# GpSimd takes shifted copies, and both score slots get a third PSUM bank, in a two-layer transformer kernel

## The chip, the cores and the metric

One NeuronCore of a Trainium2 chip runs the whole kernel. The metric is the time of one execution on the device, in microseconds (us). The work is spread over five engines: TensorE (PE in the profile, its weight loads PEld), VectorE (DVE), ScalarE (ACT), GpSimd (POOL) and the DMA queue of SyncE (SP). Each engine runs its own instructions strictly in the order in which they were written, and waits on semaphores for the others.

## The reference

Sequence length 2048, width 512, 32 heads of 16, hidden width 1792; everything bfloat16. The same attention block and the same MLP are applied twice.

```python
def _A_ref(x, wqkv, wo):
    qkv = (x @ wqkv).reshape(B, S, 3, H, Dh) ...
    scores = jnp.einsum("bhqd,bhkd->bhqk", q, k) * (Dh ** -0.5)
    p = _softmax(scores, axis=-1)
    o = jnp.einsum("bhqk,bhkd->bhqd", p, v)
    return o ... @ wo
x = x + _A_ref(_layernorm(x), A_wqkv, A_wo)
x = x + _B_ref(_layernorm(x), B_w1, B_b1, B_w2, B_b2)   # h = gelu(x @ w1 + b1); h @ w2 + b2
x = x + _A_ref(_layernorm(x), A_wqkv, A_wo)
x = x + _B_ref(_layernorm(x), B_w1, B_b1, B_w2, B_b2)
```

## The kernel before, in words

**Cells.** Attention is worked in cells. A cell is one row quarter `a` of the array, one block of 128 keys and 512 query columns: one matmul (`score`, L1137) fills one PSUM bank of 128x512 float32 with transposed scores, an exponential turns the bank into bfloat16 weights in SBUF, and a second matmul (`pvs`, L1527) with 17 columns of V (16 and a column of ones, for the softmax's denominator) adds them to the output bank. There are 4096 cells, grouped in passes of one query segment and one group of heads.

**Two ways to the exponential.** Most cells go to ScalarE (`exps`, L1466), which does two or three banks in one ACTIVATE. Cells of four chosen key blocks per layer (`KD`) can go to VectorE instead. There the exponential is made from integer arithmetic: `dfirst` (L1283) evicts the bank with one multiply and add into uint16, so that the integer is the bit pattern of a bfloat16 near the exponential. `dchain` then makes three shifted copies of it in SBUF, for one cell or a pair of cells: L1344 writes copy 1 (+32) from copy 0, L1346 writes copies 2 and 3 (+64) from copies 0 and 1. The four copies meet V and three scaled versions of V (`vc`) in four second matmuls, and their sum is the better approximation. So a cell on VectorE costs one eviction, its share of two copies, and four second matmuls instead of one.

**Banks.** PSUM has eight banks. Score slot 0 has banks 0, 1 and 2, slot 1 has banks 3 and 4, bank 5 collects the second matmuls of one pass, and banks 6 and 7 are for side work: projections, the MLP's matmuls, the output projection. Bank 7 (and bank 6, when no side work asks for it) may be lent to VectorE's cells. `scores` fills the two slots in turn, and ScalarE works on one while TensorE fills the other. `attach` adds VectorE's cells in lent banks to the group of score matmuls that fills a slot; `swap` gives the third bank of slot 0 to VectorE if VectorE is about to be free. Then ScalarE's ACTIVATE on that slot covers two banks, and the slot becomes free when both ScalarE and VectorE have read it (`slot_done`). Slot 1 is always two banks wide.

**Who writes the order.** A planner in the kernel (`_Sched.run`) holds a thread for each piece of work, a cost for each operation and a clock for each engine, and picks the operation that can start first; ties go by priority. What it picks is appended to that engine's list, with the waits that its reads and writes need (`_Prog.group`). The chip then runs these five lists as they stand: the planner's clocks decide the order and nothing else. Side work is let in when a due share of the cells has been scored (`when`, `HB`, `YB`, `JB`); `fill` puts extra matmuls into gaps on TensorE. `EARLY` is the number of head groups of layer 1's second query segment that are begun before the last key blocks of layer 1 are there. `norm` transposes a finished pass into the tile `XT`, takes reciprocals (L746), multiplies (L754, on GpSimd for most passes, else on VectorE) and transposes back (L759). GpSimd also makes the masked queries (L1085), the normalised rows (L602), the scaled V (L1068) and the layer norm's power (L588).

Of the kernel before, what the change touches and what calls it, by code (L numbers as in the profile page):

```python
# [5 lines left out]
ALU = mybir.AluOpType  # L6
# [14 lines left out]
PVB = 5  # L21
MISC = (6, 7)
# [9 lines left out]
DU = 9  # L32
# [11 lines left out]
EARLY = 4  # L44
# [17 lines left out]
CPRIO = 8  # L62
FPRIO = 1.5
# [11 lines left out]
SHIFT = 32  # L75
# [128 lines left out]

LATENCY = {"pe": 0.20, "act": 0.10, "dve": 0.10, "pool": 0.15, "sp": 0.1}


class _Sched:
# [5 lines left out]
    def __init__(self, P):  # L214
# [10 lines left out]
        self.filler, self.free, self.fills = None, None, set()  # L225

# [70 lines left out]

    def landed(self, keys):
        return max(self.end.get(self.P.lastw[k], 0.0) if k in self.P.lastw else 1e9 for k in keys)
# [34 lines left out]
    def run(self):  # L334
        while True:
# [8 lines left out]
            for th in self.threads:  # L344
# [6 lines left out]
                best.setdefault(e, []).append((th, rdy))  # L351
# [33 lines left out]
            if e == "pe":  # L385
                self.mode = op.mode
                self.note(start + cost - op.cost, start + cost, op)
            self.ops.append((e, start, cost, op.writes[0] if op.writes else ""))
# [113 lines left out]
class _Plan:  # L502
# [215 lines left out]
    def norm(self, l, seg, g, b, part, final):  # L718
# [18 lines left out]
        xt = T["XT"]  # L737
        if part:
# [9 lines left out]
        gb, ts = self.heads(seg, g)  # L748
        o = gb % 2
        pool = g < 6 and seg[2] == 512  # L750
        nb = w // 32
        for i, t in enumerate(ts):
# [4 lines left out]
                reads=["XT", "RC"], writes=["OTT.%d.%d" % (o, t)])  # L757
        if ts[-1] == 1:
            yield _Op("dve", 0.05 + 0.65 * w / 512, lambda e: e.transpose(T["OTN"][:, gb, q0:q0 + w], T["OTT"][:, o, 0:w]),  # L759
                      reads=["OTT.%d.0" % o, "OTT.%d.1" % o],  # L760
                      writes=["OTN.%d.%d" % (gb, t % 4) for t in self.tiles(seg)])
            yield ("give", ("otn", l, seg, gb))
# [262 lines left out]
    def route(self, name, b):  # L1025
# [3 lines left out]
        if self.lend == 2:  # L1029
            return "misc"  # L1030
        return "misc" if q > (0 if b == MISC[0] else QUEUE if self.scored < self.rush else RUSH) or b == MISC[0] else "dbank"

    def setup_attention(self):
# [19 lines left out]
        self.lead = [min(pi for pi, p in enumerate(self.pas) if p[0] == l) for l in range(NL)]  # L1053
        self.held, self.users = [len(x) for x in SLOTS], [0] * len(SLOTS)
# [5 lines left out]
    def vcopies(self):  # L1060
        T = self.T
        for l in range(NL):
# [9 lines left out]
            self.lend = 1  # L1072

# [16 lines left out]
    def free(self, now, ahead):  # L1090
# [3 lines left out]
        for b in (6, 7, 0, 1, 2, 3, 4, 5) if src else ():  # L1094
# [97 lines left out]
    def swap(self, op, start, cells, extra, free):  # L1192
# [11 lines left out]
        f, r = self.score(c, self.s.tokens[("qp", c[0])], SLOTS[0][2])  # L1204
# [8 lines left out]
        self.join(op, d, SLOTS[0][2], extra, free)  # L1213
# [22 lines left out]
    def scores(self):  # L1236
        u = 0
        pools = self.s.pools
        while True:
            sl = yield ("acq", "s")  # L1240
            cells = []
            for _ in SLOTS[sl]:
# [6 lines left out]
            work = list(zip(cells, SLOTS[sl]))  # L1249
# [12 lines left out]
            op.late = lambda op, start: (self.attach(op, start, cells, extra, free), self.swap(op, start, cells, extra, free))  # L1262
# [359 lines left out]
```

The softmax here doesn't subtract the row's maximum and nothing guards it: scores larger than these inputs give would overflow.

## Time and profile before

| what | value |
|---|---|
| median of 3 runs | 1588.41 us (1587.63 to 1589.98) |
| the profiled execution's own time | 1589.16 us |
| its span in the profile | 1587.3 us |
| ScalarE busy | 1547.1 us, 97% of the span |
| TensorE busy | 1424.2 us, 90% |
| VectorE busy | 1352.0 us, 85% |
| GpSimd busy | 200.5 us, 13% |
| granted TensorE clock | 0.995 |
| cells on ScalarE, on VectorE | 3207, 889 |

The cells come from the counts of the groups: 711, 96 and 82 evictions at L1283 make 889, and the rest of 4096 is ScalarE's. Busy times of one engine overlap at their ends: an ACTIVATE's record is longer than the distance to the next one's start, so the distance from start to start tells what one costs.

### The profile page before, as it was taken

The numbers are of one execution on the slowest core, as the hardware profiler recorded it, in microseconds if no ns is written. First come the engines' busy times: TensorE is split into PE (matmuls) and PEld (weight loads), VectorE is DVE, ScalarE is ACT, GpSimd is POOL, SyncE is SP. The second block draws the span as 40 slices with busy tenths as digits, with TensorE's granted clock in tenths as the row PEclk, the third lists the DMA queues.
The fourth block names the chain that finished last, engine by engine and source line by source line (L and its number), as shares of the span: only waits on it lengthen the run. The fifth ranks groups of instructions, "written<-read, shape, count | busy, mean of one in ns | idle before, by whom it ended". The sixth has DMA issues, their size and how long they took to land.

```text
span 1587.3 us, 42896 instructions
## 1 busy us (share of the span) xinstructions
PE 1424.2 (90%) x18701; PEld 444.6 (28%) x18701; DVE 1352.0 (85%) x2564; ACT 1547.1 (97%) x1393; POOL 200.5 (13%) x250
## 2 busy tenths in 40 slices
PE   8998888899999898988989998888998889898988
PEld 3222222222222222222222222222222222333344
DVE  5689999888898889978788789899878988998984
ACT  7999999999999999999999999999999999999996
POOL 5200012001100201002120020122001000010000
PEclk9999999999999999999999999999999999999999
DMA  5100001241114311143111510001251105312520
GB/s 140 22 2 1 2 14 41 77 132 46 27 45 130 85 41 28 42 140 74 36 28 48 172 44 28 1 2 33 67 167 43 28 15 151 103 36 87 155 82 29
DMA packets 141767, 96.88 MB, mean 61 GB/s; under 512 B 36877, under 2 KB 141582, under 8 KB 141582
## 3 DMA queue, kind: packets, MB, share of 16 engines
q1 hardware_dynamic: 141582, 94.14, 21.2%
q8 instruction: 149, 2.44, 0.6%
q14 instruction: 36, 0.29, 0.1%
HBM read 84.41 MB, written 2.10 MB: 55 GB/s over the span
## 4 chain that ended last, share of the span: by engine, by line
ACT 67%; PE 29%; DVE 2%; POOL 1%; issue 1%; DMA 0%; ACTq 0%; POOLq 0%
ACT pt L1466 60%; PE ps L512 11%; PE ps L1137 9%; PE ps L1527 8%; ACT g L893 3%; ACT v L1466 2%; ACT kt L1466 1%; ACT q L1466 1%; DVE du L1283 1%; ACT L893 1%; ACT L1466 0%; DMA xf<-xln 0%; PE ps L1125 0%; POOL xln L602 0%; POOL rstd L588 0%
## 5 line engine op out<-in xcount | busy, mean ns | idle before, releaser
L1466 ACT ACTIVATE pt<-ps 128x1536 bf16<-128x1536 f32 (+2 forms) x1261 | 1384.2, 1246 | 15.2 <-PE ps L1137 10.3
L1137 PE MATMUL ps<-qp,kt 32*128 32x512 bf16 x4096 | 538.0, 385 | 140.8 <-ACT pt L1466 106.7
L1283 DVE TENSOR_SCALAR du<-ps 128x512 uint16<-128x512 f32 x711 | 479.7, 685 | 97.5 <-PE ps L1137 89.6
L1527 PE MATMUL ps<-pt,v 128*17 128x512 bf16 (+1 forms) x3368 | 433.8, 359 | 2.3 <-ACT pt L1466 0.8
L1527 PE MATMUL ps<-du,vc 128*17 128x512 bf16 (+1 forms) x2394 | 333.8, 358 | 2.7 <-DVE du L1346 1.4
L1137 PEld LDWEIGHTS ps<-qp,kt 32*128 32x128 bf16 x4096 | 140.6, 91 | 685.9 <-ACT pt L1466 304.2
L1346 DVE TENSOR_SCALAR du<-du 128x2048 uint16<-128x2048 uint16 x361 | 246.3, 687 | 2.5
L1085 POOL TENSOR_SCALAR qp<-q,mask 128x512 bf16<-128x512 bf16 (+1 forms) x91 | 66.3, 728 | 1013.8 <-PE ps L1137 1005.1
L512 PE MATMUL ps<-xf,wr 128*32 128x512 bf16 (+1 forms) x2400 | 170.8, 368 | 1.7 <-DMA xf<-xln 1.1
L1527 PE MATMUL ps<-du,v 128*17 128x512 bf16 (+1 forms) x798 | 154.7, 360 | 1.7 <-DVE xt L743 0.9
L1344 DVE TENSOR_SCALAR du<-du 128x1024 uint16<-128x1024 uint16 x361 | 150.5, 428 | 2.0
L1527 PEld LDWEIGHTS ps<-pt,v 128*17 128x17 bf16 x3368 | 111.8, 89 | 113.0 <-issue 72.9
L512 PE MATMUL ps<-wr,g 128*32 128x512 bf16 x1600 | 123.8, 384 | 5.5 <-ACT g L893 5.0
L1527 PEld LDWEIGHTS ps<-du,vc 128*17 128x17 bf16 x2394 | 92.5, 89 | 62.7 <-issue 27.5
L872 DVE TENSOR_SCALAR g<-ps,hb1t 128x512 bf16<-128x512 f32 (+1 forms) x112 | 79.8, 713 | 13.8 <-PE ps L512 12.9
L1527 PE MATMUL ps<-dh,vc 128*17 128x512 bf16 (+1 forms) x321 | 90.6, 358 | 0.0
L1283 DVE TENSOR_SCALAR dh<-ps 128x512 uint16<-128x512 f32 x96 | 65.8, 685 | 11.5 <-PE ps L1137 10.8
L1283 DVE TENSOR_SCALAR kt<-ps 128x512 uint16<-128x512 f32 x82 | 56.1, 684 | 20.7 <-PE ps L1137 19.9
L512 PEld LDWEIGHTS ps<-xf,wr 128*32 128x32 bf16 x2400 | 53.6, 95 | 61.5 <-issue 33.5
L602 POOL TENSOR_SCALAR xln<-x,rstd,nmr 128x512 bf16<-128x512 bf16 x58 | 58.2, 1008 | 33.3 <-DMA xf<-xln 23.2
L754 POOL TENSOR_TENSOR ott<-xt,rc 128x256 bf16<-128x256 f32 x42 | 29.5, 703 | 178.5 <-DVE rc L746 178.5
L1125 PE MATMUL ps<-vc 128*32 128x512 bf16 x476 | 50.9, 395 | 0.1
(93 smaller groups left out, 1185.2 us busy)
## 6 DMA issues: line engine op xcount, KB each, us to landing
wr<-in_B_w_dram SPq DMA_DIRECT2D x256, 256.0 KB, 2.9
wr<-in_A_wqkv_dram SPq DMA_DIRECT2D x24, 256.0 KB, 2.9
wr<-in_A_wo_dram SPq DMA_DIRECT2D x18, 256.0 KB, 2.9
out_dram<-x SPq DMA_DIRECT2D x16, 128.0 KB, 2.7
g<-in_A_wqkv_dram SPq DMA_DIRECT2D x3, 512.0 KB, 5.1
x<-in_A_x_dram SPq DMA_DIRECT2D x3, 512.0 KB, 8.0
q<-in_B_w_dram SPq DMA_DIRECT2D x3, 512.0 KB, 3.9
kt<-in_B_w_dram SPq DMA_DIRECT2D x4, 256.0 KB, 3.3
```

Source lines behind the costliest of these rows:

```text
L512: return [lambda e, a=a: e.matmul(out[32 * a:32 * a + 32, :], lhsT=lhsT[:, 32 * a:32 * a + 32], rhs=rhs, start=start, stop=stop, tile_posi ...
L602: yield _Op(eng, cost, lambda e: e.tensor_scalar(T["XLN"][:, x, :], T["X"][:, t, :], T["RSTD"][:, t:t + 1], T["NMR"][:, t:t + 1], op0=ALU. ...
L872: yield _Op("dve", 0.21 + n / 966, lambda e, fc=fc, pb=pb: e.tensor_scalar(T["G"][:, fc, q], pb, T["HB1T"][:, fc:fc + 1], None, op0=ALU.ad ...
L893: lambda e, g=g: e.activation(out=g, in_=g, func=ACT.Gelu_apprx_tanh), reads=gk, writes=gk, prio=2)
L1085: yield _Op("pool", 0.1 + 0.6 * w / 512, lambda e, s=s, q=q, i=i, t=t, w=w: e.tensor_scalar(T["QP"][:, s, w * i:w * i + w], q, T["MASK"][: ...
L1125: fns.append(lambda e, o=o, w=w, a=a, m=m: e.matmul(o, lhsT=w, rhs=rhs, start=start, stop=start, tile_position=(0, m * a)))
L1137: return (lambda e: e.matmul(o, lhsT=lhsT, rhs=rhs, start=True, stop=True, tile_position=(32 * a, 0)), ["K%d.%d.%d" % (l, gb, kt // 4), "Q ...
L1283: yield _Op("dve", 0.68, lambda e: e.tensor_scalar(u, self.bank(b), E_SCALE, E_BIAS, op0=ALU.mult, op1=ALU.add), reads=["B.%d" % b], write ...
L1344: yield _Op("dve", 0.08 + 0.14 * n, lambda e: e.tensor_scalar(U[:, 1, 0:n, :], U[:, 0, 0:n, :], SHIFT, None, op0=ALU.add), reads=key[0], w ...
L1346: yield _Op("dve", 0.08 + 0.28 * n, lambda e: e.tensor_scalar(U[:, 2:4, 0:n, :], U[:, 0:2, 0:n, :], 2 * SHIFT, None, op0=ALU.add), reads=k ...
L1466: yield _Op("act", 0.065 + 0.4267 * n, lambda e, src=src, dst=dst: e.activation(out=dst, in_=src, func=ACT.Exp, scale=0.25), reads=["B.%d" ...
L1527: op.fns.append(lambda e, o=o, lhsT=q[0][0][m], rhs=q[0][1][:, n * m:n * m + n], a=a, st=st, sp=sp: e.matmul(o, lhsT=lhsT, rhs=rhs, start= ...
```

## The change

It has five parts, all in the planner's input; the operations themselves stay, but for the engine of one.

1. **Shifted copies on GpSimd.** Copy 1 (L1344 before, L1381 after) is written for GpSimd when GpSimd's planned clock is more than 0.5 us behind VectorE's (`SPARE`), else for VectorE. Copies 2 and 3 (L1346, then L1384) stay on VectorE (`WHOLE` is False). An eviction is L1318 after, an exponential L1508, a second matmul L1569.
2. **Locks in the plan.** `locking` and `unlocked` keep windows in which GpSimd's operations, and VectorE's SBUF-to-SBUF copies, are taken to exclude each other; such an operation's start is put off to the end of the other's window, so another one may be picked first.
3. **Banks.** Slot 0 keeps 0, 1 and 2. Slot 1 keeps 3 and 4 and gets bank 5 once the first scaled V is made (`widen`). The collecting bank is 6. Bank 7 is left for side work and for VectorE. `swap` may give the third bank of either slot to VectorE.
4. **Norm.** `XT` and the two halves of `OTT` are taken and given back as a whole, so that one pass's norm doesn't begin in them while another's is being planned.
5. **`EARLY`** goes from 4 to 2.

The diff, cut to its core:

```diff
-PVB = 5
-MISC = (6, 7)
+WIDE = 5
+PVB = 6
+MISC = (7, 5)
...
-EARLY = 4
+EARLY = 2
...
+SPARE = -0.5
+WHOLE = False
...
+HOLD = (0.05, 0.13)
...
+    def locking(self, op):
+        w = op.writes[0] if op.writes else ""
+        if op.eng == "pool":
+            return not w.startswith("RSTD")
+        return op.eng == "dve" and (w.startswith("XLN") or w.startswith("DU") and w.split(".")[2] != "0")
+
+    def unlocked(self, op, rdy):
+        if op.eng not in self.locks or not self.locking(op):
+            return rdy
+        now = t = max(rdy, self.clock[op.eng])
+        for a, b in self.locks["pool" if op.eng == "dve" else "dve"]:
+            if a <= t < b and not (op.eng == "dve" and a >= self.fast[0] and t < self.fast[1] + 0.02):
+                t = b
+        return t if t > now else rdy
...
-                best.setdefault(e, []).append((th, rdy))
+                best.setdefault(e, []).append((th, self.unlocked(th.op, rdy)))
...
+            if self.locking(op):
+                self.fast = (start, start + cost) if e == "dve" else self.fast
+                self.locks[e] = self.locks[e][-3:] + [(start + HOLD[0], start + cost - HOLD[1])]
...
+        gb, ts = self.heads(seg, g)
+        yield ("acq", "xt")
...
+        if ts[0] == 0:
+            yield ("take", ("ott", o))
...
+        yield ("rel", "xt", 0)
...
+            yield ("rel", "ott", o)
...
+        if b == WIDE:
+            return "wide"
...
+        self.slots = [list(x) for x in SLOTS]
...
+            if WIDE in self.s.pools["misc"]:
+                self.s.pools["misc"].remove(WIDE)
+                self.s.pools["wide"].append(WIDE)
...
-        f, r = self.score(c, self.s.tokens[("qp", c[0])], SLOTS[0][2])
+        f, r = self.score(c, self.s.tokens[("qp", c[0])], self.slots[sl][2])
...
-        if b in MISC:
+        if b == MISC[0]:
             yield ("rel", "dbank", b)
         else:
-            yield from self.slot_done(0)
+            yield from self.slot_done(0 if b < 3 else 1)
...
-        yield _Op("dve", 0.08 + 0.14 * n, lambda e: e.tensor_scalar(U[:, 1, 0:n, :], U[:, 0, 0:n, :], SHIFT, None, op0=ALU.add),
+        clock = self.s.clock
+        eng, fix, one = ("pool", 0.1, 0.65) if clock["pool"] < clock["dve"] + SPARE else ("dve", 0.08, 0.14)
+        yield _Op(eng, fix + one * n, lambda e: e.tensor_scalar(U[:, 1, 0:n, :], U[:, 0, 0:n, :], SHIFT, None, op0=ALU.add),
                   reads=key[0], writes=key[1])
...
+    def widen(self):
+        yield ("acq", "wide")
+        self.slots[1].append(WIDE)
...
+        s.spawn(self.widen(), 4)
```

## The prediction

> **What bounds the kernel now.** I read the busy times first, then the groups by form, then the order of ScalarE's instructions in time, then the waits, and last the spread of durations of single tiles.
>
> ```profile
> PE 1424.2 (90%) x18701; PEld 444.6 (28%) x18701; DVE 1352.0 (85%) x2564; ACT 1547.1 (97%) x1393; POOL 200.5 (13%) x250
> ACT 67%; PE 29%; DVE 2%; POOL 1%; issue 1%; DMA 0%; ACTq 0%; POOLq 0%
> ```
>
> ScalarE is busy 97% of the span and holds two thirds of the chain that ended last. TensorE's 29% of the chain is mostly stretches in which it runs without a gap beside ScalarE. The exponentials, kept apart by form:
>
> ```profile
> L1466 ACT ACTIVATE pt<-ps 128x1024 bf16<-128x1024 f32 x769 | 798.2, 1080 | 7.4 <-PE ps L1137 6.0
> L1466 ACT ACTIVATE pt<-ps 128x1536 bf16<-128x1536 f32 x491 | 740.2, 1507 | 7.8 <-PE ps L1137 4.2 <-PE ps L1527 1.3
> ```
>
> With those that write into kt, v and q there are 540 three-bank and 793 two-bank ACTIVATEs, and one of one bank. Their records overlap, so the cost is read from start to start, in the timeline of ScalarE:
>
> ```profile
> 346.30 1.48 ACT L1466 ACTIVATE kt<-ps 128x1536 bf16<-128x1536 f32 x1
> 347.63 1.07 ACT L1466 ACTIVATE pt<-ps 128x1024 bf16<-128x1024 f32 x1
> 348.53 1.51 ACT L1466 ACTIVATE kt<-ps 128x1536 bf16<-128x1536 f32 x1
> 349.87 11.48 ACT L1466 ACTIVATE pt<-ps 128x1024 bf16<-128x1024 f32 x10
> ```
>
> 347.63 - 346.30 = 1.33 and 348.53 - 347.63 = 0.90. Over the whole trace the medians are 1.331 and 0.904 us: a bank costs 0.427 us and an instruction 0.05 us. What lies above these medians is a bubble. I summed it: 42.3 us behind two-bank and 4.6 us behind three-bank ACTIVATEs, 47 us in all. A two-bank one covers TensorE's turn (free slot, scores, semaphore) badly, a three-bank one nearly always.
>
> ```profile
> PEld ps L1137 <- ACT pt L1466: 304.2, 598, 2.0
> PEld ps L1137 <- DVE du L1283: 89.6, 152, 1.6
> DVE du L1283 <- PE ps L1137: 89.6, 180, 3.1
> ```
>
> The scores wait mostly for ScalarE (304 us). VectorE has 235 us of idle time, most of it waiting for scores, so it isn't the bound. Outside the exponentials there are 12.3 us before the first one and 26.7 us after the last.
>
> **What the Trainium skill says.** "SBUF — State Buffer", section "Who interferes with whom": VectorE in a two-port mode and GpSimd share a port pair; whoever issues first has it and the other fully blocks. The trace agrees:
>
> ```profile
> L1344 DVE TENSOR_SCALAR du<-du x361: 228/418/1067, 68.7 to 1557.5; 128x1024 uint16<-128x1024 uint16 x175, 128x512 uint16<-128x512 uint16 x6
> L1346 DVE TENSOR_SCALAR du<-du x361: 382/683/1107, 70.2 to 1557.9; 128x2048 uint16<-128x2048 uint16 x175, 128x1024 uint16<-128x1024 uint16 x6
> L1283 DVE TENSOR_SCALAR du<-ps x711: 646/690/694, 65.6 to 1554.5; 128x512 uint16<-128x512 f32 x178
> L1085 POOL TENSOR_SCALAR qp<-q,mask x91: 476/694/1487, 12.7 to 1492.4; 128x512 bf16<-128x512 bf16 x75, 128x256 bf16<-128x256 bf16 x16
> ```
>
> The columns are minimum, median and maximum in ns. Copies go from 418 to 1067 and from 683 to 1107, GpSimd's masked queries from 694 to 1487. "VectorE: DVE Perf Modes", section "Why PSUM operands drop a tier", says that a PSUM operand leaves only one port; so evictions shouldn't block, and they never pass 694. "GPSIMD Engine Reference", section "3.1 Elementwise", gives some 1.8 cycles an element as the best case, 768 ns for 512 elements; the trace has 694 for L1085 there.
>
> **The change part by part.** The counts come from the order of instructions that the changed planner writes.
>
> *ScalarE's work.* VectorE's cells go from 889 to 921, so ScalarE's from 3207 to 3175. There are now 599 three-bank and 689 two-bank ACTIVATEs: 599 x 1.331 + 689 x 0.904 = 1420.2, against 540 x 1.331 + 793 x 0.904 + 0.8 = 1436.4. That is -16.2 us, on the bound. The gelus, table loads and copies are as before.
>
> *VectorE.* Of 512 first copies 357 go to GpSimd (313 of 1024 elements, 44 of 512). VectorE's first copies fall from 194.9 us (150.5 + 27.2 + 17.2 in three groups) to 96 x 0.418 + 59 x 0.284 = 57. The 32 new evictions cost 32 x 0.685 = 22, the extra second copies some 11. Sum -105 us, worth nothing by itself: VectorE is off the path. It is what lets 32 more cells in.
>
> *GpSimd.* No row of before shows this copy. From 256 to 512 elements L1085 goes from 482 to 694 ns undisturbed, so 1024 take 1.12 us by that slope; the page's 1.8 cycles at the 1.2 GHz it states give 1.54 us. I take 1.3 between them: 313 x 1.3 + 44 x 0.7 = 438 us, and GpSimd goes from 200 to some 640 us, 41%. Masked queries and normalised rows now queue behind copies; they are made well ahead (L1085 idled 1005 us for a free buffer), so nothing is late.
>
> *The port.* Before, 123 copies on VectorE met a GpSimd operation begun earlier, and by their means (548, 777 and 305 ns against 417, 682 and 283) lost 13.5 us. GpSimd's busy time grows 3.2 times, its operations (0.8 us on average, the copies 1.3) some 1.5 times in length, VectorE's copies fall from 996 to 667. Unplanned that makes 13.5 x 3.2 x 1.5 x 0.67 = 43 us; if the planned windows hold, nearly nothing. It hits VectorE, not ScalarE.
>
> *The new wait.* L1384 must now wait on VectorE for GpSimd's copy, and the evictions queued behind it wait too; those evictions free score banks. Between the eviction that releases a copy and the wait for it the new order puts a median of 2.9 us of VectorE work. If the copy lands 1.2 us after its release, the places with less cover cost 14 us of VectorE's time; at 1.8 us, 49 us.
>
> *Gated slots, the disputed term.* Before, 124 of 1334 slot turns waited for a VectorE eviction in the slot's own third bank. Behind a two-bank ACTIVATE such turns had a mean bubble of 92 ns (27 of 124 were released late by VectorE), the others 45 ns; behind a three-bank one the mean was 7 ns, none of them gated. Afterwards 671 turns that follow an exponential are gated: 368 behind two banks, 303 behind three; ungated are 321 and 296. The bounds for a gated turn are 45 (the gate is harmless) and 92 behind two banks, 7 and 54 behind three (the same 47 on top, though 0.43 us more cover should take over half of it: 25). I take 70 and 15, since VectorE is less loaded but less punctual: 321 x 0.045 + 368 x 0.070 + 296 x 0.007 + 303 x 0.015 = 46.8 us. Against 46.9 that is nothing. The low bounds give 35 us (-12); 92 and 25 give 58 (+11), 92 and 54 give 67 (+20).
>
> *One bank for side work.* Its 272 evictions and the matmuls before them now take turns in bank 7. In the opening two places in the new order become late: the score group after cell 151 waits for the eviction of the first keys of chunk 3 (two projection groups of eight matmuls, 0.45 us each by the 108 in 6.01 us near the end of the chain, a second copy of 0.68 and the eviction of 0.69 stand in front, and one ACTIVATE of 0.9 covers them), and after cell 199 an exponential waits for second matmuls behind a V eviction. About 2 and 1.5 us, +3.5. At the turn to layer 1 the keys of chunk 3 stand 72 cells ahead of their first use (164 before), which at 0.378 us a cell (1548 us from the first exponential to the last, over 4096) is 27 us, so `EARLY` = 2 costs nothing; without that cover a post-processing chain would stand on the path.
>
> *TensorE.* 102 more second matmuls, four at a time in 0.22 us, are 5.6 us beside 944 fillers of some 95 us: hidden. After the last exponential 12 more stand ahead of the last transpose, +0.6.
>
> *Norm.* Taking `XT` whole delays one pass's transpose at most until the last one's multiply; passes are some 24 us apart. Nothing.
>
> Sum: -16.2 - 0.1 + 3.5 + 0.6 = -12.2 us. The profiled execution took 1589.16 us (its span 1587.3 and 1.9 around it) and lies 0.75 above the median, so: 1589.2 - 12.2 = 1577.0, less 0.75, 1576.
>
> **The rivals.** (1) *The gate is harmless*: VectorE has 105 us more room and hits its marks. Bubbles 35 us, sum -24, 1564. For it: 33 of 60 gated turns that VectorE released last had no bubble. (2) *The gate at its full price*, 92 and 25: bubbles 58 us, sum -1, 1587, the same within measurement (0.2%, 3.2 us, is about what can be told from no change). (3) *Slower: VectorE stands behind GpSimd.* A copy on GpSimd lands late or holds the port, L1384 stands at the head of VectorE's queue, the eviction behind it comes late and with it either slot; both slots are open to it now, one before. VectorE's lateness is up to 49 + 43 = 92 us. My sum stays a gain until 12 us of it reach ScalarE (13%); at a quarter, 23 us, the time is 1599. For it: copies reach 1.1 us where they meet GpSimd. Against: a slot's eviction has most of the other slot's ACTIVATE as slack. That the change doesn't do what it says is excluded by the order: 357 copies stand on GpSimd, banks 2 and 5 have 334 and 341 evictions.
>
> **How the numbers follow.** My forecast, around 1576 (1569 to 1585): 0.45. Rival 1: 0.24. Rival 2: 0.10. Rival 3: 0.21. Faster by over 0.2% is the first two, 0.69; within 0.2% 0.10; slower 0.21. The range goes from 1560, some 4 us under rival 1, to 1595, into rival 3, and leaves out the rest.
>
> **What would show it.** Right: 1288 exponentials at unchanged 1.33 and 0.90 us from start to start, bubbles of 40 to 55 us, GpSimd busy some 640 us, evictions at 690 ns still. Wrong: copies on GpSimd over 1.8 us; VectorE waits for GpSimd of over 50 us; bubbles behind gated turns well above 92 ns; or an idle stretch of ScalarE at the turn to layer 1.

## The result and the profile after

The changed kernel takes 1730.67 us (median of 4 runs, 1727.22 to 1733.69) against 1588.66 us for the kernel before on the same chip: a ratio of 1.0893, 95% interval 1.0868 to 1.0918. It is 9% slower, and far outside the predicted range of 1560 to 1595. The profiled execution took 1733.69 us, its span is 1731.9, the granted clock 0.963.

Busy times and the shares of the chain that ended last, of the kernel after:

```profile
PE 1460.2 (84%) x18803; PEld 439.6 (25%) x18803; DVE 1356.4 (78%) x2263; ACT 1551.6 (90%) x1347; POOL 1175.7 (68%) x605
...
DVE 31%; POOL 28%; PE 24%; ACT 14%; issue 2%; DMA 1%; SPq 0%; POOLq 0%; DVEq 0%; ACTq 0%
```

ScalarE held 67% of the chain before and holds 14% now. GpSimd went from 1% to 28%, VectorE from 2% to 31%. GpSimd is busy 1176 us where some 640 were forecast. The spread of durations (minimum, median, maximum in ns) of the copies and evictions, from the tile `du` after:

```profile
L1318 DVE TENSOR_SCALAR du<-ps x741: 630/682/693, 66.5 to 1696.8; 128x512 uint16<-128x512 f32 x186
L1384 DVE TENSOR_SCALAR du<-du x375: 384/694/2985, 71.4 to 1702.0; 128x2048 uint16<-128x2048 uint16 x183, 128x1024 uint16<-128x1024 uint16 x5
L1381 POOL TENSOR_SCALAR du<-du x291: 1486/2771/3652, 68.4 to 1700.5; 128x1024 uint16<-128x1024 uint16 x142, 128x512 uint16<-128x512 uint16 x4
```

This is the line to read first. A first copy on GpSimd takes 2.77 us in the median, not 1.3. Where nothing of VectorE lay beside them, 1024 elements took 2.77 and 512 took 1.49 us, which is 2.50 ns an element and 0.21 us fixed. VectorE's evictions stay at 0.68 us and never pass 693 ns, but its second copies (L1384) now reach 2985 ns, 1107 before. That longest one is a single case, and no copy of GpSimd's made it: it met the one MEMSET with which GpSimd fills a column of V. From the timelines of the two engines (start, length):

```profile
237.63 2.98 DVE L1384 TENSOR_SCALAR du<-du 128x2048 uint16<-128x2048 uint16 x1
237.78 2.29 POOL L561 MEMSET v<- 128x512 bf16 x1
```

No other copy on VectorE is more than 0.87 us over its undisturbed length. Next the waits of the kernel after (who waits, for whom: us in total, times, longest):

```profile
PEld ps L1172 <- ACT pt L1508: 180.8, 349, 1.9
PEld ps L1172 <- DVE du L1318: 176.2, 266, 2.9
...
DVE du L1384 <- POOL du L1381: 137.5, 112, 2.9
ACT pt L1508 <- PE ps L1172: 128.0, 185, 3.2
...
PEld ps L1569 <- POOL du L1381: 52.9, 60, 2.3
```

The third line didn't exist before: with the same wait on the tiles `kt` and `dh`, VectorE stands 151 us for GpSimd's copies, and 168 us for GpSimd in all. The scores now wait nearly as long for VectorE's evictions (176 us, 90 before) as for ScalarE, and ScalarE waits for scores: 128 us on this row. The last line is a second way for the delay: TensorE's second matmuls stand for GpSimd's copies themselves, and scores are queued behind them. How it goes in one place, from the timeline of VectorE (start, length, in brackets the idle time before and its releaser):

```profile
701.74 0.68 DVE L1318 TENSOR_SCALAR du<-ps 128x512 uint16<-128x512 f32 x1
703.66 0.69 DVE L1384 TENSOR_SCALAR du<-du 128x2048 uint16<-128x2048 uint16 x1 [1.25 <-POOL du L1381]
704.27 0.75 DVE L901 TENSOR_SCALAR g<-ps,hb1t 128x512 bf16<-128x512 f32 x1
704.93 0.68 DVE L1318 TENSOR_SCALAR du<-ps 128x512 uint16<-128x512 f32 x1
```

GpSimd's copy ran from 700.86 for 2.77 us to 703.63. VectorE had 1.35 us of other work in that time (701.07 to 702.42), then stood 1.25 us at L1384; the eviction at 704.93 stood behind it. A stretch of the chain a little later shows this reaching ScalarE (start, length, what):

```profile
712.58 2.92 POOL du L1381
715.50 1.46 POOL dh L1381
716.96 6.37 POOL du L1381 x2
723.35 0.69 DVE du L1384
724.04 0.60 DVE du L1318
724.64 0.67 DVE g L901
725.36 1.05 PE ps L536 x16
726.40 0.35 PE ps L1172 x3
726.77 3.29 ACT pt L1508 x3
```

Four copies back to back on GpSimd (10.75 us), then what stood behind the last of them: the second copy on VectorE, an eviction and an MLP bias (`g`) queued after it, the MLP matmuls that needed that, the scores behind these on TensorE, and the exponential.

ScalarE's time, summed from start to start as in the prediction, tells where the 144.6 us of span (1731.9 - 1587.3) are:

| us | before | after |
|---|---|---|
| exponentials at 1.331 and 0.904 | 1436.4 | 1420.1 |
| bubbles behind two banks | 42.3 | 128.4 |
| bubbles behind three banks | 4.6 | 76.4 |
| after the last exponential | 26.5 | 29.1 |

The 16 us of saved work are there. Bubbles took 158 us. Of those after, 121 are longer than 0.6 us and hold 140 us; before there were 10 with 9 us.

### The profile page after: what moved, and what is told of

It is laid out like the page before. It is cut to its first block, busy times and chain, and to the rows that moved or that the text cites. A ratio compares the mean times of both kernels' runs of the same rounds, so it can differ in the third digit from the quotient of the medians.

```text
span 1731.9 us, 43259 instructions
## 1 busy us (share of the span) xinstructions
PE 1460.2 (84%) x18803; PEld 439.6 (25%) x18803; DVE 1356.4 (78%) x2263; ACT 1551.6 (90%) x1347; POOL 1175.7 (68%) x605
## 4 chain that ended last, share of the span: by engine, by line
DVE 31%; POOL 28%; PE 24%; ACT 14%; issue 2%; DMA 1%; SPq 0%; POOLq 0%; DVEq 0%; ACTq 0%
POOL du L1381 23%; ACT pt L1508 13%; DVE du L1318 10%; DVE du L1384 9%; PE ps L536 9%; PE ps L1569 8%; PE ps L1172 7%; POOL kt L1381 3%; DVE g L901 2%; DVE dh L1384 1%; DVE kt L1384 1%; DVE du L1381 1%; POOL xln L626 1%; DVE kt L1318 1%; DVE dh L1318 1%
## 5 line engine op out<-in xcount | busy, mean ns | idle before, releaser
L1508 ACT ACTIVATE pt<-ps 128x1024 bf16<-128x1024 f32 (+1 forms) x1215 | 1384.2, 1238 | 142.5 <-PE ps L1172 128.0
L1381 POOL TENSOR_SCALAR du<-du 128x1024 uint16<-128x1024 uint16 (+1 forms) x291 | 827.4, 2848 | 371.5 <-DVE du L1318 349.9
L1172 PE MATMUL ps<-qp,kt 32*128 32x512 bf16 x4096 | 524.9, 394 | 146.2 <-ACT pt L1508 69.0
L1318 DVE TENSOR_SCALAR du<-ps 128x512 uint16<-128x512 f32 x741 | 497.2, 682 | 88.0 <-PE ps L1172 84.9
L1569 PE MATMUL ps<-pt,v 128*17 128x512 bf16 (+1 forms) x3330 | 449.9, 369 | 21.4 <-POOL du L1381 10.4
L1384 DVE TENSOR_SCALAR du<-du 128x2048 uint16<-128x2048 uint16 (+1 forms) x375 | 312.9, 840 | 138.2 <-POOL du L1381 137.5
L1569 PE MATMUL ps<-du,vc 128*17 128x512 bf16 (+1 forms) x2487 | 358.0, 371 | 24.0 <-DVE du L1384 14.8
L1569 PE MATMUL ps<-du,v 128*17 128x512 bf16 (+1 forms) x829 | 162.7, 371 | 21.9 <-POOL du L1381 13.2
L1569 PEld LDWEIGHTS ps<-pt,v 128*17 128x17 bf16 x3330 | 112.1, 89 | 145.8 <-issue 76.5
L1569 PEld LDWEIGHTS ps<-du,vc 128*17 128x17 bf16 x2487 | 94.3, 90 | 91.1 <-DVE du L1384 30.8
L1381 POOL TENSOR_SCALAR kt<-kt 128x1024 uint16<-128x1024 uint16 x29 | 84.2, 2904 | 42.2 <-DVE kt L1318 42.1
L1120 POOL TENSOR_SCALAR qp<-q,mask 128x512 bf16<-128x512 bf16 (+1 forms) x89 | 76.7, 861 | 53.1 <-PE ps L1172 43.9
L1569 PE MATMUL ps<-dh,vc 128*17 128x512 bf16 (+1 forms) x315 | 89.7, 364 | 7.3 <-POOL du L1381 4.0
L1381 POOL TENSOR_SCALAR dh<-dh 128x512 uint16<-128x512 uint16 x37 | 61.3, 1657 | 23.5 <-DVE dh L1318 22.0
L1318 DVE TENSOR_SCALAR dh<-ps 128x512 uint16<-128x512 f32 x94 | 64.1, 682 | 11.2 <-PE ps L1172 10.7
L1318 DVE TENSOR_SCALAR kt<-ps 128x512 uint16<-128x512 f32 x86 | 58.7, 683 | 8.8 <-PE ps L1172 7.6
```

What stands on the lines that cost most here:

```text
L1120: yield _Op("pool", 0.1 + 0.6 * w / 512, lambda e, s=s, q=q, i=i, t=t, w=w: e.tensor_scalar(T["QP"][:, s, w * i:w * i + w], q, T["MASK"][: ...
L1172: return (lambda e: e.matmul(o, lhsT=lhsT, rhs=rhs, start=True, stop=True, tile_position=(32 * a, 0)), ["K%d.%d.%d" % (l, gb, kt // 4), "Q ...
L1318: yield _Op("dve", 0.68, lambda e: e.tensor_scalar(u, self.bank(b), E_SCALE, E_BIAS, op0=ALU.mult, op1=ALU.add), reads=["B.%d" % b], write ...
L1381: yield _Op(eng, fix + one * n, lambda e: e.tensor_scalar(U[:, 1, 0:n, :], U[:, 0, 0:n, :], SHIFT, None, op0=ALU.add), reads=key[0], write ...
L1384: yield _Op(eng, fix + 2 * one * n, lambda e: e.tensor_scalar(U[:, 2:4, 0:n, :], U[:, 0:2, 0:n, :], 2 * SHIFT, None, op0=ALU.add), reads=k ...
L1508: yield _Op("act", 0.065 + 0.4267 * n, lambda e, src=src, dst=dst: e.activation(out=dst, in_=src, func=ACT.Exp, scale=0.25), reads=["B.%d" ...
```

## Experiments

Three theories; the expectations call them theory 1, 2 and 3. *Size*: GpSimd's copy in this form is 2.1 times as long as taken, VectorE's queue stands behind it, and everything else is as forecast. *Banks*: the two shared slots cost most of it and the copies only join in. *Port*: what hurts isn't the wait but that GpSimd's long operations hold the port that VectorE's copies need. Each ratio is to the kernel before on the same chip, with its 95% interval. "Lost" is the time of VectorE above the undisturbed 417, 683 and 283 ns of its copies, and its waits for GpSimd; before it is 13.3 + 3.0 us.

**All copies on VectorE, the rest of the change kept** (`e1_vector_copies`).

```diff
-SPARE = -0.5
+SPARE = -1e9
```

> The change without its first part: all 506 first copies stay on VectorE and the rest is as changed (locks in the plan, three banks in both slots, one bank for side work, XT whole, EARLY 2). VectorE gets 911 cells, 616 three-bank and 668 two-bank exponentials, 1423.8 us at 1.331 and 0.904. Theory 1 (the slow copy on GpSimd is the loss): 1565 to 1590, bubbles of 35 to 60 us. Theory 2 (gated slots and one bank for side work are the loss): 1680 or more, with bubbles of 150 us or more. Theory 3 (the shared port is the loss): 1565 to 1590 as in theory 1.

Measured: 1595.56 us, 1.0040 (1.0025 to 1.0054). Exponentials 1423.8, bubbles 62.1, tail (the time after the last exponential) 29.1, lost 14.9 + 5.3. That is some 6 us above the range of theory 1. Locks, banks, norm and `EARLY` together cost 0.4%, although 911 cells on VectorE (889 before) take 12.6 us off ScalarE. They aren't the 9%.

**The copies alone, on the banks of before** (`e2_copies_alone`): parts 1 and 2 in the kernel before, 357 of 507 copies on GpSimd. Without part 4 a pass's norm may read the `XT` of the next pass; the number and kind of the operations are not touched by that.

```diff
+        clock = self.s.clock
+        eng, fix, one = ("pool", 0.1, 0.65) if clock["pool"] < clock["dve"] + SPARE else ("dve", 0.08, 0.14)
-        yield _Op("dve", 0.08 + 0.14 * n, ...
+        yield _Op(eng, fix + one * n, ...
```

> The kernel before with the first two parts of the change alone: 357 of 507 first copies on GpSimd, locks in the plan; banks, norm and EARLY as before. VectorE gets 904 cells, 152 of them in slot 0's third bank, exponentials 1429.9 us. If the slow copy is the loss with any banks: 1680 to 1740. If the loss needs the gated slots of the new banks to reach ScalarE: 1600 to 1650.

Measured: 1730.38 us, 1.0884 (1.0862 to 1.0905); bubbles 188, lost 93.4 + 179.1. The copies alone lose all of it, on banks that nobody moved. *Banks* is out.

**What sets a copy's length** (`p1_forms`, `p2_forms`). After the last result GpSimd runs sixteen forms of a copy on one tile of 1024 elements, with nothing of VectorE beside them; `p1` adds ten of them to the changed kernel, `p2` six more to the one before. The first four lines here are from `p1`, the last is from `p2`:

```diff
+            yield _Op("pool", 2.0, lambda e: e.tensor_scalar(o, u, SHIFT, None, op0=ALU.add), **kw)
+            yield _Op("pool", 2.0, lambda e: e.tensor_scalar(o, u, SHIFT, 0, op0=ALU.add, op1=ALU.add), **kw)
+            yield _Op("pool", 2.0, lambda e: e.tensor_scalar(ob, ub, 1.0, None, op0=ALU.mult), **kw)
+            yield _Op("pool", 2.0, lambda e: e.tensor_scalar(o, u, 1, 1, op0=ALU.mult, op1=ALU.mult), **kw)
...
+            yield _Op("pool", 2.0, lambda e: e.tensor_scalar(o, u, 1, SHIFT, op0=ALU.mult, op1=ALU.add), **kw)
```

> The changed kernel with thirty GpSimd operations of 128x1024 elements added after the last result, three of each of ten forms, with VectorE idle; their outputs go nowhere. In the changed kernel the copy (uint16, one addition) takes 2.77 us undisturbed, the masked query (bfloat16, two multiplications by a scalar) 0.69 for half the elements. If the number type is what costs, every uint16 form takes 2.5 us or more, and the bfloat16 forms 1.1 to 1.3. If the form with one operation is what costs, uint16 with two additions takes 1.1 to 1.4 and bfloat16 with one operation 2.5 or more. If the addition is what costs, bfloat16 additions are slow as well.

> The kernel before, with eighteen GpSimd operations of 128x1024 uint16 added after the last result, three of each of six forms. So far a multiplication by an immediate followed by another took 1.04 us, a single addition 2.77, a single multiplication 2.78, two additions 3.64. If multiplications alone have a fast routine, a multiplication followed by an addition or a subtraction takes 2.7 or more. If the fast routine is for any two operations that start with a multiplication, those take 1.04 and an addition followed by a multiplication takes over 2.7. A pointer in place of the immediate should change nothing.

The groups on GpSimd at the end of `p1` (busy us and mean ns after the bar); L1453 is +32 alone, L1454 is +32 and +0, L1455 a bfloat16 multiplication alone, L1459 two multiplications of uint16, L1461 a plain copy:

```profile
L1455 POOL TENSOR_SCALAR du<-du 128x1024 bf16<-128x1024 bf16 x2 | 5.6, 2782 | 0.2
...
L1454 POOL TENSOR_SCALAR du<-du 128x1024 uint16<-128x1024 uint16 x1 | 3.6, 3639 | 0.1
L1453 POOL TENSOR_SCALAR du<-du 128x1024 uint16<-128x1024 uint16 x1 | 2.8, 2772 | 0.1
L1459 POOL TENSOR_SCALAR du<-du 128x1024 uint16<-128x1024 uint16 x2 | 2.1, 1044 | 0.2
...
L1461 POOL COPY du<-du 128x1024 uint16<-128x1024 uint16 x2 | 2.1, 1037 | 0.1
```

And of `p2`: L1411 is times 1 and +32, L1413 times 1 and -32, L1414 times a value from SBUF (as in the masked queries) and +32, L1415 that multiplication alone:

```profile
L1415 POOL TENSOR_SCALAR du<-du,mask 128x1024 uint16<-128x1024 uint16 x2 | 5.7, 2849 | 0.2
...
L1413 POOL TENSOR_SCALAR du<-du 128x1024 uint16<-128x1024 uint16 x1 | 3.6, 3640 | 0.1
L1414 POOL TENSOR_SCALAR du<-du,mask 128x1024 uint16<-128x1024 uint16 x1 | 1.1, 1122 | 0.1
L1411 POOL TENSOR_SCALAR du<-du 128x1024 uint16<-128x1024 uint16 x1 | 1.0, 1047 | 0.1
```

Neither the number type nor the addition makes a copy long. A single operation takes 2.77 to 2.85 us (`p1` tried it in both types); two multiplications, or a multiplication and an addition in either order, take 1.04 to 1.12; two additions, or a multiplication and a subtraction, 3.64. So an instruction that does more takes 38% of the time, and the same copy can be had in 1.05 us by multiplying by 1 first. (The listings begin inside the three rounds, so some forms show fewer counts.)

**The same order, only the copy's length changed** (`e4_two_ops`, `e5_fast_standin`, `e6_mult_add`). The planner's prices stay, so all instructions stand where they stand after; `e5` leaves +32 out of GpSimd's copies, `e4` and `e6` compute what the kernel does. The lines are shortened: each new form stands behind a test that the copy is GpSimd's, and VectorE's copies keep the single addition.

```diff
-e.tensor_scalar(U[:, 1, 0:n, :], U[:, 0, 0:n, :], SHIFT, None, op0=ALU.add)
+e.tensor_scalar(U[:, 1, 0:n, :], U[:, 0, 0:n, :], SHIFT, 0, op0=ALU.add, op1=ALU.add)    # e4
+e.tensor_scalar(U[:, 1, 0:n, :], U[:, 0, 0:n, :], 1, 1, op0=ALU.mult, op1=ALU.mult)      # e5
+e.tensor_scalar(U[:, 1, 0:n, :], U[:, 0, 0:n, :], 1, SHIFT, op0=ALU.mult, op1=ALU.add)   # e6
```

> The changed kernel in the same order, but the copy on GpSimd is written with two additions (32, then 0), the result being the same. If the form with one operation is what costs, a copy takes 1.1 to 1.5 us and the whole 1560 to 1590, which also tests the other terms of the prediction. If the number type or the addition costs, a copy takes 2.7 us or more and the whole 1725 to 1740. Theory 3 (port): a copy of 1.3 us still blocks, and the time stays above 1650.

> The changed kernel in the same order, but GpSimd's copy is two multiplications by 1, which leaves out the addition of 32 in the copies that GpSimd makes, so it only stands in for a copy that costs 1.04 us. Theory 1 (the price of the copy is the loss): 1570 to 1592, gated turns behind two banks 60 to 95 ns, VectorE's waits for GpSimd under 20 us. Theory 3 (the port blocks whatever the price): 1620 or more, with bubbles of 100 us or more.

> The changed kernel in the same order, GpSimd's copy written as a multiplication by 1 and an addition of 32. If a leading multiplication is what is fast, as e5: 1570 to 1592 with copies of 1.04 us. If only two multiplications are fast, copies of 3.6 us and about 1950, as with two additions.

| | copy, us | time, us | ratio | bubbles | lost |
|---|---|---|---|---|---|
| e6 | 1.05 | 1593.61 | 1.0023 (1.0015 to 1.0032) | 67.6 | 40.8 + 7.9 |
| e5 | 1.05 | 1592.41 | 1.0020 (1.0012 to 1.0028) | 62.6 | 41.4 + 7.9 |
| after | 2.77 | 1730.67 | 1.0893 (1.0868 to 1.0918) | 204.8 | 106.2 + 167.8 |
| e4 | 3.63 | 1951.51 | 1.2288 (1.2261 to 1.2315) | 422 | 99.7 + 355.5 |

With one order, one set of banks and the same 357 copies on GpSimd, the time follows the copy's length: *size* is shown. From 1.05 to 2.77 us it costs 137 us, from there to 3.63 another 221. `e4` fell outside every range of its time: the second addition was expected to shorten the copy or leave it, and it lengthened it. The tile `du` of `e6`:

```profile
L1384 DVE TENSOR_SCALAR du<-du x375: 386/683/1536, 71.1 to 1561.8; 128x2048 uint16<-128x2048 uint16 x183, 128x1024 uint16<-128x1024 uint16 x5
L1381 POOL TENSOR_SCALAR du<-du x291: 620/1047/1472, 68.1 to 1560.3; 128x1024 uint16<-128x1024 uint16 x142, 128x512 uint16<-128x512 uint16 x4
```

But even so it is 0.2% slower than before, and 2 us above its own range, where the forecast with a slower copy of 1.3 us was a gain of 12 us. That is a second miss, taken up below.

**The planner told the true price** (`e3_true_price`): it had 1.4 us for a copy of 1024 elements, the chip takes 2.77.

```diff
-("pool", 0.1, 0.65)
+("pool", 0.21, 1.28)
```

> The change with the planner's price of a GpSimd copy raised from 0.1 + 0.65 n to 0.21 + 1.28 n, the 1.49 and 2.77 us that were measured. The order is planned anew: 259 copies go to GpSimd, VectorE gets 874 cells, exponentials 1440.1 us. Theory 1 as a wrong price in the plan: most of the loss goes, 1580 to 1610. Theory 1 as a slow copy whatever the order: 1650 or more. Theory 2: 1680 or more.

Measured: 1631.15 us, 1.0268 (1.0252 to 1.0284), with 259 copies on GpSimd and 874 cells on VectorE; bubbles 77, lost 72.1 + 13.5. An order made for the true length avoids the waits (168 to 13.5 us) but has less work to move (exponentials 1440.1) and pays at the port. The time lies between its ranges: the bad order is a large part of the loss, not all.

**Wait or port** (`e12_port_only`, `e13_slow_no_wait`, `e15_fast_no_wait`). `e12` is `e1` with 1360 additions of 192 elements on GpSimd (0.69 us each, GpSimd busy 1300 us) that write a tile nobody reads: the port, and no wait for a copy, though in pieces a quarter as long as the slow copy. (VectorE still waits 26 us, 5 in `e1`, for other steps that queue behind the additions.) In `e13` VectorE makes copies 2 and 3 from copy 0 (+64, +96), so that it need not wait for GpSimd's slow copy 1; `e15` is that with the fast copy.

```diff
+        src = self.T["VC"][:, 0, 0, 0:192].bitcast(U16)                                 # e12
+        fn = lambda e: e.tensor_scalar(self.T["SCR"][:, :], src, SHIFT, None, op0=ALU.add)
+        for _ in range(2 * n):
+            yield _Op("pool", 0.05 + 0.325, fn, reads=["VC.0.0"], writes=["SCR"])
...
+        if eng == "pool":                                                                # e13, e15
+            for i in (2, 3):
+                yield _Op("dve", 0.08 + 0.14 * n, lambda e, i=i: e.tensor_scalar(U[:, i, 0:n, :], U[:, 0, 0:n, :], i * SHIFT, None, op0=ALU.add), reads=key[0], writes=key[i])
```

> The change with all first copies on VectorE (as the run without the first part), and beside them 1360 GpSimd additions of 192 elements, 0.69 us each, some 940 us as GpSimd's copies have in the changed kernel. They write a tile that nobody reads, so nobody waits for them: only the shared port is left of the slow copy. VectorE has 903 cells and exponentials of 1427.3 us. If the loss comes from engines that wait in their order for a slow copy, 1595 to 1625. If it comes from VectorE's copies being held by the port, 1680 or more, with VectorE's second copies at a mean of 0.9 us or more.

> The changed kernel with its slow copy, but where GpSimd makes copy 1, VectorE makes copies 2 and 3 in two instructions from copy 0 (+64 and +96), so that it never waits for GpSimd; 361 copies on GpSimd, VectorE 907 cells, exponentials 1425.7. The port is used as before. If VectorE's waiting in its order is what carries the loss to ScalarE: 1620 to 1650, near the run with the port alone (1627). If TensorE's waits for the slow copy and for its buffers do it as well: 1680 or more.

> The same order of instructions with the fast copy (1.05 us). VectorE has no wait for a copy, and 361 pairs cost it two instructions of 0.42 in place of one of 0.68. If the wait is what is left of the loss with a fast copy: 1578 to 1588. If the port is: 1590 to 1597.

| | time, us | ratio | bubbles | port + wait, us |
|---|---|---|---|---|
| e12 | 1627.25 | 1.0232 (1.0211 to 1.0253) | 91 | 68.4 + 26.3 |
| e13 | 1700.06 | 1.0706 (1.0690 to 1.0721) | 163 | 211.1 + 18.3 |
| e15 | 1607.40 | 1.0113 (1.0100 to 1.0126) | 73 | 123.1 + 1.3 |

`e12` is 2 us above its first range. It puts 32 us on `e1`, and more than two thirds of VectorE's further loss in it is at the port (53 of 75 us). `e13` took away 150 us of wait and got back 30 us of time, while the stretch doubled from 106 to 211 us: 168 us of it lie in the copies that no longer wait (L1385), which are two instructions where the changed kernel has one. So on VectorE the port took two thirds of the wait back. It isn't the whole of what is left: TensorE's weight loads still wait 30 us for GpSimd's copies in `e13` (59 after), and `e13` doesn't tell the two apart. `e15` is above both its ranges, for the same reason: the wait is gone and the stretch is 123 us, 41 in `e6`. The tile `du` of `e13`:

```profile
L1385 DVE TENSOR_SCALAR du<-du x598: 231/426/1286, 71.5 to 1662.5; 128x1024 uint16<-128x1024 uint16 x196, 128x512 uint16<-128x512 uint16 x4
```

At most 1286 ns where 417 is undisturbed, beside GpSimd copies of 2.77 us. Over all copies on VectorE 383 of 1010 are stretched, by 0.55 us on average; after, 207 of 667. "SBUF — State Buffer", section "Who interferes with whom", says of VectorE in a two-port mode and GpSimd that the one that issues first has the shared ports for its whole instruction and the other is fully blocked. For the slow copy the traces don't agree. Where a VectorE copy begins at the start of GpSimd's it stands 0.84 us; where it begins in the middle it isn't held; where it begins 0.9 us before the end it stands again. First a start from the timelines of after, then a middle and an end from `e13`:

```profile
1542.11 2.76 POOL L1381 TENSOR_SCALAR du<-du 128x1024 uint16<-128x1024 uint16 x1
1542.17 1.25 DVE L1384 TENSOR_SCALAR dh<-dh 128x1024 uint16<-128x1024 uint16 x1 [0.78 <-POOL dh L1381]
...
1514.01 2.76 POOL L1381 TENSOR_SCALAR du<-du 128x1024 uint16<-128x1024 uint16 x1
1514.96 0.41 DVE L1385 TENSOR_SCALAR du<-du 128x1024 uint16<-128x1024 uint16 x1
1515.89 1.16 DVE L1385 TENSOR_SCALAR du<-du 128x1024 uint16<-128x1024 uint16 x1
```

In all of `e13`, 499 copies on VectorE began inside a GpSimd copy of 1024 elements, and none was stretched by more than 0.87 us; the 154 of them that began with 1.2 to 1.8 us of it left were not stretched at all. So the slow copy takes 2.6 times as long as the fast one (2.77 and 1.05 us), but blocks only in two stretches of some 0.9 us, where the fast one blocks nearly throughout (a copy that begins with it in `e6` stands 0.85 us). *Port* is a part of the loss and in part takes the wait's place. Alone and in short pieces it made 32 us (`e12`); no run has the slow copy's port with no wait for a copy anywhere, so its share of the 137 us isn't measured.

**Is there a version that beats before?** All with the fast copy of `e6`: `e7` on the old banks with parts 1, 2 and 4; `e8` with `EARLY` 4; `e10` with that and a price near the true one; `e14` is `e10` with both copies on GpSimd.

```diff
-("pool", 0.1, 0.65)
+("pool", 0.06, 0.49)            # e7, e10, e14
-EARLY = 2
+EARLY = 4                       # e8, e10, e14
-WHOLE = False
+WHOLE = True                    # e14: copies 2 and 3 too, as 1, 2 * SHIFT, op0=ALU.mult, op1=ALU.add
```

> The kernel before with parts 1, 2 and 4 of the change and a fast copy (a multiplication by 1 and an addition of 32, 1.05 us), priced in the plan at 0.06 + 0.49 n: 397 of 505 first copies on GpSimd, old banks, EARLY 4. VectorE gets 902 cells, exponentials 1430.2 (5.4 less). If the new banks ate the gain (gated slots, one bank for side work): bubbles of 40 to 50 us as before and 1580 to 1587. If GpSimd's copies cost something even when fast: 1590 or more.

> The changed kernel with the fast copy and EARLY back at 4, planned anew at the changed kernel's price: 360 copies on GpSimd, VectorE 916 cells, exponentials 1422.4. If EARLY 2 is behind the two bubbles of 3.2 and 1.3 us at the turn to layer 1, these go and the whole is 1588 to 1593, 2 us less than with EARLY 2 after 2.3 us more of exponentials. If they come from the one bank for side work, they stay and the whole is 1594 or more.

> The changed kernel with the fast copy, its true price in the plan (0.06 + 0.49 n) and EARLY 4: 397 of 515 copies on GpSimd, VectorE 931 cells, exponentials 1415.1 (20.5 less than before). My terms for gated turns, opening and tail give bubbles of 60 us and 1582 to 1588. If the bubbles grow with every cell that goes to VectorE: 1590 to 1597.

> The changed kernel with the fast form for all three copies of 246 of 520 pairs on GpSimd (WHOLE), its true price in the plan and EARLY 4: for these pairs VectorE neither waits for GpSimd nor runs a copy that needs the port. VectorE 935 cells, exponentials 1413.6, 22 less than before. If port and wait are what ate the gain: bubbles of 45 to 55 us and 1570 to 1585. If gated slots and the one bank for side work are: 1588 or more.

| | time, us | ratio | exponentials | bubbles | lost | tail |
|---|---|---|---|---|---|---|
| e7 | 1600.16 | 1.0066 (1.0046 to 1.0086) | 1430.2 | 62.5 | 43.9 + 36.9 | 26.6 |
| e8 | 1593.47 | 1.0026 (1.0014 to 1.0037) | 1422.4 | 66.5 | 40.4 + 8.3 | 26.3 |
| e10 | 1595.08 | 1.0031 (1.0019 to 1.0043) | 1415.1 | 74.4 | 37.1 + 22.6 | 26.5 |
| e14 | 1597.02 | 1.0057 (1.0044 to 1.0070) | 1413.6 | 77.1 | 88.4 + 1.4 | 26.3 |

None does. Each takes up to 23 us of work off ScalarE and gives at least as much back in bubbles. `e14` has the least work on ScalarE and hardly a wait; it loses 88 us at the port, beside fast copies of 2048 elements that take 1.90 us and stretch VectorE's by up to 1.85. Its range of 1588 or more was to speak for the slots and banks, but with that loss in it the run doesn't decide.

## Why the prediction was wrong

**The step that failed** is the price of GpSimd's copy: "From 256 to 512 elements L1085 goes from 482 to 694 ns undisturbed, so 1024 take 1.12 us by that slope; the page's 1.8 cycles at the 1.2 GHz it states give 1.54 us. I take 1.3 between them". It measured 2.77 us, outside both bounds: the slope and the estimate from the page. L1085 was taken as the nearest row, but it is two multiplications and the copy one addition, and on GpSimd these are different cases. The slope was good for its own form: 1.12 by it, 1.122 in `p2`'s L1414. The page ("GPSIMD Engine Reference", "3.1 Elementwise") names its 1.8 cycles a best case, and I used a best case as an upper bound. The code of before gave a hint that I passed over. Every TENSOR_SCALAR on GpSimd there has two operations, the first of them a multiplication, and in L1068 and L1085 the second does nothing:

```python
src, w, 1.0, op0=ALU.mult, op1=ALU.mult
q, T["MASK"][:, t:t + 1], 1.0, op0=ALU.mult, op1=ALU.mult
```

No row of before showed a single operation there, so the upper bound had no ground.

**The mechanism** was named: it is rival 3, VectorE stands behind GpSimd, with the links it gives. One link more is TensorE's own wait for GpSimd's copies (59 us of its weight loads after). Its size was not named. It allowed up to 92 us of lateness and 13% to 25% of it on ScalarE. After, VectorE loses 258 us more than before and ScalarE's bubbles grow by 158, 61%. Over the runs, in us:

| run | VectorE lost | bubbles |
|---|---|---|
| before | 16 | 47 |
| e1 | 20 | 62 |
| e6 | 49 | 68 |
| e10 | 60 | 74 |
| e7 (old banks) | 81 | 62 |
| e3 | 86 | 77 |
| e14 | 90 | 77 |
| e12 | 95 | 91 |
| e15 | 124 | 73 |
| e13 | 229 | 163 |
| e2 (old banks) | 273 | 188 |
| after | 274 | 205 |
| e4 | 455 | 422 |

From `e6` to `e3`, `e14` and `e12` a quarter to a half of the further loss gets through, to `e15` only 5 of 75 us; from `e12` to after, 114 of 179 us; from after to `e4` 217 us of bubbles for 181 of loss, more than all (TensorE's granted clock falls to 0.896 there as well). So there is no one rate: a quarter is fair for the small losses, and too low by more than half for the large ones. The orders differ between these runs, so where a loss falls counts as well as its size. The bubbles of `e1` don't come from this loss; they belong to the second miss.

**The copies' own sums.** That the trace before agrees with a full block was read too quickly: 50 copies on VectorE began there with 0.75 us or more of a GpSimd operation left, and only one of them, beside the MEMSET, was stretched by more than 0.03 us. The port's sum, "Unplanned that makes 43 us", was near for a copy of about the assumed length (`e6`: 40.8, 13.3 before) and 106 at the true one. That is in part luck: with the operations of `e6`, shorter than assumed, the same product gives some 31 (13.5 x 2.9 x 1.2 x 0.67). The wait, "14 us" at 1.2 us, was 7.9 in `e6`. VectorE's -105 us held but for the port: the lengths of its instructions sum to 74 us less in `e6` (1422 against 1497), after the port has taken 28 back. (Its busy time, in which records overlap at their ends, falls by 54, from 1352 to 1298.) That it is "worth nothing by itself" held. GpSimd's 640 us were 574 in `e6`. That masked queries and rows are made well ahead held nearly: after, the rows have 1% of the chain and the queries none in its list of lines.

**The rest, read from `e6`**, where the copy is out of the way. Its span is 1594.3, +7.0 against the forecast of -12.2.

- ScalarE's work, -16.2: right (-16.3), at 1.331 and 0.905 us.
- Turns, "Against 46.9 that is nothing", and opening, +3.5: wrong by 17 us. Bubbles are 67.6. By the planned order of slots and the starts in the trace, gated turns have a mean of 77 ns behind two banks and 25 behind three (70 and 15 taken), ungated ones 65 and 32 (45 and 7 taken), so the larger miss is in the turns that were thought unchanged. Only without the bubbles above 0.6 us do the gated means come to 62 and 14; but the means from before held such long bubbles too, 8.9 us in all. Short ones went from 38.0 to 46.4 us, and long ones from 8.9 (10 of them) to 21.2 (18 of them).
- The opening's two places: 1.64 and 2.84 us, 4.5 together, right in place and nearly in size.
- "`EARLY` = 2 costs nothing": wrong in the tail, by 2.6 us (below), and open at the turn to layer 1. There ScalarE stands in `e6`, for second matmuls that must free a buffer:

```profile
1003.46 3.82 ACT L1508 ACTIVATE pt<-ps 128x1536 bf16<-128x1536 f32 x3
1010.28 6.39 ACT L1508 ACTIVATE pt<-ps 128x1536 bf16<-128x1536 f32 x5 [3.00 <-PE ps L1569]
```

- That bubble of 3.25 us from start to start and another of 1.27 make 4.5 us. I had counted cells between a key's making and its use, but no key is late here: the second matmuls wait for the addition at the end of a pass (L765, on VectorE from 1008.03), which frees the collecting bank and stands behind four second copies in VectorE's queue. `e8` with `EARLY` 4 has neither bubble, but 2.3 us more of exponentials and as long a time; `e1`, also with `EARLY` 2, has neither as well. So it is this order that makes them, and not `EARLY` = 2 alone.
- The tail, +0.6: 2.6 (before, it is 26.5 by the records, not 26.7). The chain holds 480 matmuls of side work there in both kernels (136 and 344 in `e6`, 108 and 372 before). But in `e6` the normalisation of the last rows stands between the two parts, 2.8 us from 1575.89 to 1578.70, where before it is 0.55 us of transposes. I had counted second matmuls alone. `e8` has the chain of before and a tail of 26.3, and `e7`, `e10` and `e14`, with `EARLY` 4 as well, 26.3 to 26.6; `e1`, with `EARLY` 2, has 29.1 as `e6`.

These sum to -16.3 + 20.7 + 2.6 = 7.0, which is what the span shows. So with the copy priced at 1.05 I should still have called a gain, and been wrong by 19 us; `e1`, without any copy on GpSimd, has the same surplus (bubbles +15.2, tail +2.6, work -12.6).

**Open.** Why the turns with three-bank slots have more bubbles isn't settled; without the opening and the turn to layer 1 it is some 12 us in `e6`. As much is there with all copies on VectorE (`e1`), so GpSimd isn't needed for it. In `e1` it can be placed: 362 gated turns behind two banks have a mean of 97 ns, which is rival 2's full price of 92 and not my 70 (10 us), and 321 ungated ones behind three banks 24 ns for 7 (5 us). Why those, and why `e6` has 77 and 32 on these kinds, no run tells. `e7` on the old banks has as many bubbles, but with 81 us lost at the port and in waits, where `e1` has 20. No run kept the old banks with 921 cells and an undisturbed VectorE.

## What to carry to other kernels

An operation moved to another engine is priced from a row of the same form there, operations and all; if none exists, a few of them at the end of the kernel tell the price in one run, and a best case is no upper bound. An engine that is off the path but whose queue frees the path's buffers has slack to lose, here some tens of microseconds in 1590; after that more than half of its lateness goes through. Removing a wait for another engine's result gains little where the next instruction needs a port that this engine holds: of 150 us of wait that `e13` took away, 105 came back at the port.

## What the runs showed of the hardware

- GpSimd's TENSOR_SCALAR on 128x1024 two-byte elements takes 1.04 to 1.12 us with two multiplications or a multiplication and an addition, 2.77 to 2.85 with either alone, 3.64 with two additions or a multiplication and a subtraction. uint16 or bfloat16 makes no difference. A plain copy takes 1.04. The fast forms are under the estimate of 1.54 us that I had as the upper bound, the single operation is 80% over it.
- A GpSimd copy of 2.77 us (one operation) holds up VectorE's SBUF copies in its first and its last part alone: by at most 0.87 us over 499 meetings in `e13`, and not at all in the 154 that began with 1.2 to 1.8 us left. In `e4` (3.63 us a copy) it was at most 0.89 us. The fast copy of 1.05 us held those that began with it by 0.85 us (`e6`). GpSimd's MEMSET of 2.29 us held one by 2.30 us.
- VectorE's evictions from PSUM were not touched by any of this: at most 694 ns in every run, beside GpSimd operations of up to 3.6 us. That agrees with "VectorE: DVE Perf Modes", section "Why PSUM operands drop a tier": a PSUM operand leaves VectorE a single port.
- The granted TensorE clock was 0.995 before, 0.963 after and 0.896 in `e4`, with 47, 205 and 422 us of bubbles. It doesn't follow the bubbles strictly: `e2` has 0.976 with 188 us, `e13` 0.968 with 163.
